# Second buffers for the first block's softmax, an early table load, and two new figures in a list scheduler

## The chip, the cores and the metric

The kernel runs on one core of one Trainium2 chip. A core has a matrix engine (PE, with its weight loads PEld), a vector engine (DVE), a scalar engine (ACT), a general engine (POOL) and a sync engine (SP) that here issues every transfer between device memory and the on-chip memory. Each engine executes its own instructions in the order in which they were written. The metric is the device time of one execution in microseconds (us); lower is better.

## What is computed

Three stages follow each other on 8 sequences of 576 tokens with 512 features, all in float32:

```python
# 1: attention inside chunks of 64 tokens, 8 heads of 64
scores = (q_c @ k_c.T) / 8;  attn = softmax(scores);  x = attn @ v_c
# 2: gated MLP with a convolution over the tokens
h = relu(x @ w_in)                      # 512 -> 1024
h = h * sigmoid(conv3(h, conv_w))
x = h @ w_out                           # 1024 -> 512
# 3: Fourier mixing, norm, MLP
u = x + real(fft over tokens and features of x)
out = u + relu(norm(u) @ w_ch1) @ w_ch2 # 512 -> 2048 -> 512
```

## The kernel before

**The stages.** The 4608 tokens are cut into ten blocks, of 256, eight times 512, and 256 tokens. For each block `attention(i, q, ...)` computes the heads in two halves, q = 0 and q = 1, and `values` multiplies by V; then come eight feature groups f, each with an `m_step` (times `w_in`, relu, convolution, gate) and an `x_step` (times `w_out`). Finished sequences are folded and transformed (`fold`, `d_step`, `s_step`, `u_step`). About 560 us into the execution the first two stages end, and two long stretches of matrix products for stage three follow (`group` with line L946, `second` with line L1010).

**The weights.** They arrive as 64-bit words in which two 32-bit words stand for one number, 512 KB for one group. `load_weight` loads the 16 groups of `w_in` and `w_out` in turn into five landing buffers (names `dd`, `fw`, `wide` in the trace), and `to_float32` turns each into float32 with one ACT multiplication (L293) and three DVE operations (L294, L295, L296). For the first block the float32 weights are used as they are (L460, L532); later blocks use a split into a high and a low part (L280 on ACT, L281 on DVE).

**The softmax of one half.** PE makes the scores (L393); DVE takes the maxima (L398) and scales them (L399) into `mx`; ACT computes the exponentials row by row into `es`, with sums into `sm` (L404); DVE adds a small number to the sums (L408), takes reciprocals (L409) and multiplies (L410); PE transposes `es` (L419), ACT copies the result to `at` (L422); PE multiplies by V (L436), ACT copies that out (L443). In the kernel before, `es`, `mx` and `sm` have one buffer each, so the second half's exponentials are written where the first half's were.

**The order of the work.** No order is written out. Every step is given to a `Plan` with an engine, an assumed cost, a priority number and the buffers that it reads and writes. `Plan.emit` is a list scheduler: it keeps an assumed clock for each engine, picks the next step by earliest start and then by priority, and emits the instructions of each engine in that order. The order is fixed before the kernel runs; at run time the engines wait for each other by semaphores alone. Two figures in it:

```python
o.end = t + o.cost * (2 if e == "PE" and t < self.COLD else 1)     # PE at double cost up to COLD ns
...
moved = max(o.end + 1500, moved) + o.nbytes / 280                  # all transfers in one row, 280 bytes per ns
o.lat = moved + 300 - o.end
```

`cv` is a pair of buffers of the convolution, 512 columns wide, used in turn by the `m_step`s.

Of the kernel before, what the change touches and what calls it, by code (L numbers as in the profile page):

```python
# [8 lines left out]
F32 = mybir.dt.float32  # L9
# [3 lines left out]
ACT = mybir.ActivationFunctionType  # L13
# [88 lines left out]
class Plan:  # L102


    CROSS = 200.0
    COLD = 30000.0
    SAME = {"DVE": 125.0, "ACT": 150.0}
    ANY_ORDER = ("o", "sum")

# [3 lines left out]
    def buf(self, pool, tag, bufs, shape, dtype=F32):  # L113
        return Buf(self, pool, tag, bufs, shape, dtype)
# [41 lines left out]
    def emit(self):  # L156
        clock, ready = {}, {}
        free = {tag: [0.0] * ring[0].bufs for (_, tag), ring in self.rings.items() if tag in self.ANY_ORDER}

        def push(o):  # L160
            ready.setdefault(o.eng, []).append(o)
            clock.setdefault(o.eng, 0.0)

        def start(o):
            t = max(o.ready, clock[o.eng])
            if o.slots:
                f = free[o.slots[0].tag]
                n = len(o.slots) + o.spare
                t = max(t, f[n - 1]) if len(f) >= n else float("inf")
            return t  # L170

        for o in self.ops:
            if not o.left:
                push(o)
        done, moved = 0, 0.0
        while True:
            best = None
            for e, ops in ready.items():
                if ops:
                    t = min(start(o) for o in ops)  # L180
                    if best is None or t < best[0]:
                        best = (t, e)
            if best is None:
                break
            t, e = best
            o = min((o for o in ready[e] if start(o) <= t), key=lambda o: (o.prio, o.seq))
            ready[e].remove(o)
            for b in o.slots:
                free[b.tag].pop(0)
            o.end = t + o.cost * (2 if e == "PE" and t < self.COLD else 1)  # L190
            clock[e] = o.end
            o.lat = 0.0
            if o.nbytes:
                moved = max(o.end + 1500, moved) + o.nbytes / 280
                o.lat = moved + 300 - o.end
            o.fn()
            done += 1
            for b in o.held:
                b.left -= 1
                if not b.left:  # L200
                    free[b.tag].append(o.end + o.lat + self.CROSS)
                    free[b.tag].sort()
            for u in o.users:
                if u.deps[o]:
                    u.ready = max(u.ready, o.end + o.lat + (self.CROSS if u.eng != e else self.SAME.get(e, 0.0)))
                else:
                    u.ready = max(u.ready, t)
                u.left -= 1
                if not u.left:
                    push(u)  # L210
        assert done == len(self.ops), (done, len(self.ops))
        return max(clock.values())
# [15 lines left out]
def kernel(  # L228
# [15 lines left out]
    pe, dve, act, pool, sp = nc.tensor, nc.vector, nc.scalar, nc.gpsimd, nc.sync  # L244
    plan = Plan()
    buf, op = plan.buf, plan.op
# [4 lines left out]
    const = ctx.enter_context(tc.tile_pool(name="const", bufs=1))  # L251
# [4 lines left out]
    pools["s"] = tc.alloc_tile_pool(name="seq", bufs=1, side="right")  # L256

    ident = const.tile([128, 128], F32, name="ident")

    def dram_buf(name, cols=512):  # L260
        b = buf("dram", name, 1, None)
        b.tile = dram.tile([128, cols], F32, name=name, tag=name)
        return b
# [6 lines left out]
    def load(dst, src, nbytes, prio, r=(), after=()):  # L270
        return op("SP", 450, lambda: sp.dma_start(out=dst(), in_=src()), prio, r=r, w=[dst], after=after, nbytes=nbytes)

    def vop(n, fn, prio, r, w, fast=False, scalars=0):
        return op("DVE", dve_cost(n, fast, scalars), fn, prio, r=r, w=w)

    def aop(n, fn, prio, r, w, psum=False, scalars=0, after=()):
        return op("ACT", act_cost(n, psum, scalars), fn, prio, r=r, w=w, after=after)
# [93 lines left out]
    def attention(i, q, prio, last):  # L371
        nw = SIZE[i] // 256
        n = 4 * nw
        blk = AT[i] // 256
        half = (slice(0, 64), slice(64, 128))
        qks, v = [], []
        for p in range(2):
            qks.append(buf(*(("s", "xlo", 2) if i + q == 1 and not i else ("a", "qk", 2)), [128, nw, 2, 256]))
            load(qks[p], lambda p=p: qk[blk:blk + nw, 2 * q + p].rearrange("w r a t -> r w a t"), 262144 * nw, prio - 12 + p)
        for p in range(2):  # L380
            v.append(buf("a", "v", 4, [128, nw, 256]))
            load(v[p], lambda p=p: v_in[blk:blk + nw, 2 * q + p].rearrange("w r t -> r w t"), 131072 * nw, prio - 10 + p)

        s = [buf("ps", "o" if i else "x", 4, [128, n, 64]) for _ in range(2)]

        def qk_unit():
            for w in range(nw):
                for j in range(2):
                    for p in range(2):
                        for u in range(2):  # L390
                            for h in range(2):
                                t, ks = qks[p](), slice(64 * (2 * j + u), 64 * (2 * j + u) + 64)
                                pe.matmul(s[h]()[half[u], 4 * w + 2 * p + j, :], t[half[h], w, 0, ks], t[half[h], w, 1, ks], start=True, stop=True)  # L393

        op("PE", 310 + 470 * nw, qk_unit, prio, r=qks, w=s)
        es, mx, sm = buf("a", "es", 1, [128, 2 * n, 64]), buf("a", "mx", 1, [128, 2, n]), buf("a", "sm", 1, [128, 2 * n, 1])
        for h in range(2):
            vop(64 * n, lambda h=h: dve.tensor_reduce(out=mx()[:, h, :], in_=s[h](), op=ALU.max, axis=AX.X), prio, [s[h]], [mx])  # L398
        vop(2 * n, lambda: dve.tensor_scalar(mx(), mx(), -0.125, None, op0=ALU.mult), prio, [mx], [mx])  # L399

        for h in range(2):
            def exp(ks, h=h):
                for k in ks:
                    act.activation(out=es()[:, n * h + k, :], in_=s[h]()[:, k, :], func=ACT.Exp, scale=0.125, bias=mx()[:, h, k:k + 1], accum_out=sm()[:, n * h + k, :])  # L404

            for ks in (range(k, k + 4) for k in range(0, n, 4)):
                op("ACT", 291 * 4, lambda exp=exp, ks=ks: exp(ks), prio, r=[s[h], mx], w=[es, sm])
        vop(2 * n, lambda: dve.tensor_scalar(sm(), sm(), 1e-9, None, op0=ALU.add), prio, [sm], [sm])  # L408
        vop(2 * n, lambda: dve.reciprocal(out=sm(), in_=sm()), prio, [sm], [sm])  # L409
        vop(128 * n, lambda: dve.tensor_tensor(es(), es(), sm().to_broadcast([128, 2 * n, 64]), op=ALU.mult), prio, [es, sm], [es])  # L410

        at = buf("a", "at", 2, [128, n, 128])
        for c in range(nw):
            tps = buf("ps", "o", 4, [128, 4, 128])

            def tr_unit(c=c, tps=tps):
                flat = es().rearrange("p a k -> p (a k)")
                for k in range(4):
                    pe.transpose(tps()[:, k, :], flat[:, 512 * c + 128 * k:512 * c + 128 * k + 128], ident)  # L419

            op("PE", 436, tr_unit, prio + 2, r=[es], w=[tps], spare=1)
            aop(512, lambda c=c, tps=tps: act.copy(out=at()[:, 4 * c:4 * c + 4, :], in_=tps()), prio + 2, [tps], [at], True)  # L422

        return lambda: values(i, q, nw, v, at, last)
# [616 lines left out]
    for q in range(2):  # L1041
        attention(0, q, -10 + q, -6 + q)()
# [8 lines left out]
    for i in range(NBLK):  # L1051
        t, u, step = place(i, 0), place(i + 1, 0) if i + 1 < NBLK else 0, SIZE[i] / 288
        if i + 1 < NBLK:
            rest = [attention(i + 1, q, *((t + (u - t) * (0.05 + 0.4 * q), u - 1.5 + 0.3 * q) if i else (t - 3.5 + 3 * q, t + 0.5 + 3 * q))) for q in range(2)]
            if not i:
                heads(1)
                for finish in rest:
                    finish()
# [54 lines left out]
    for c in range(NCH):  # L1113
        t = start + span * c
        begun = []
        for g in range(FG):
            begun.append(group(c, g, t + 7 * g))
            if (c, g) in LATE:
                n = LATE.index((c, g))
# [8 lines left out]
            second(c, j, t + 7 * (TILE0[c] // 2 + j), c + j == 0, c == NCH - 1 and j == HT[c] - 1)  # L1128

    with tc.manual_schedule():  # L1130
        make_identity(nc, ident)
        plan.emit()
        pools["e"].tile([128, 24], F32, tag="pad", name="pad", bufs=1)
        pools["e"].release()
        pools["b"].release()
# [109 lines left out]
```

## Time and profile before

| | |
|---|---|
| median of 3 runs | 1303.25 us (1302.99 to 1304.23) |
| time of the profiled execution | 1303.06 us |
| span of the profiled execution, first to last instruction | 1301.3 us |
| PE busy | 1274.9 us (98% of the span) |
| PEld busy | 1106.4 us (85%) |
| DVE busy | 1036.1 us (80%) |
| ACT busy | 761.4 us (59%) |
| granted PE clock, mean | 0.999 of full speed |
| moved by transfers | 206.16 MB |

Busy time is the time in which an instruction of that engine was executing; the rest of the span the engine waited or had nothing to do. An engine that is busy nearly all the span sets the time, and the places where it is not busy are where time could be saved.

### The profile page before, as it was taken

What the parts mean: (1) busy time and instruction counts of PE and PEld (TensorE: products, weight loads), DVE (VectorE), ACT (ScalarE), POOL (GpSimd) and SP (SyncE); (2) the same over time, 40 slices, a digit from 0 to 9 for tenths busy, and PEclk for the clock granted to TensorE, in tenths of its full rate; (3) what the DMA queues carried; (4) which work ended last, traced back from release to release, by engine and by line L of the source; (5) the groups of instructions that cost most, each with busy time, mean ns of one, the idle gap of its engine ahead of it and who ended that gap; (6) DMA issues with size and microseconds to landing.
All of it is one profiled execution on the core that took longest, in us unless ns stands there. A gap on an engine that the chain in (4) does not pass through costs nothing.

```text
span 1301.3 us, 24089 instructions
## 1 busy us (share of the span) xinstructions
PE 1274.9 (98%) x8880; PEld 1106.4 (85%) x8880; DVE 1036.1 (80%) x1909; ACT 761.4 (59%) x1902; POOL 112.3 (9%) x247
## 2 busy tenths in 40 slices
PE   5899999999999999999999999999999999999998
PEld 4788888888888888999999888888888888888887
DVE  5998878888786877887977757664599998998995
ACT  6887666768676665666756556566644334334331
POOL 0131212121030312210000000000000000000000
PEclk9999999999999999999999999999999999999999
DMA  9535242534413132258674866778655554554541
GB/s 339 178 108 175 78 129 90 187 100 158 135 57 103 34 98 62 63 172 267 203 238 144 255 182 204 214 238 273 200 159 165 176 168 146 173 171 141 174 140 41
DMA packets 155319, 206.16 MB, mean 158 GB/s; under 512 B 10304, under 2 KB 103104, under 8 KB 155200
## 3 DMA queue, kind: packets, MB, share of 16 engines
q1 hardware_dynamic: 155200, 204.61, 49.7%
q8 instruction: 70, 1.15, 0.4%
q14 instruction: 49, 0.40, 0.1%
HBM read 130.51 MB, written 74.06 MB: 157 GB/s over the span
## 4 chain that ended last, share of the span: by engine, by line
PE 93%; DVE 5%; ACT 1%; issue 1%; DMA 0%; SPq 0%; DVEq 0%; ACTq 0%
PE x L946 21%; PE x L1010 15%; PE x L538 15%; PE o L469 14%; PE o L1010 12%; PE o L946 4%; PE o L672 3%; PE o L705 2%; PE o L727 1%; PE o L436 1%; PE o L393 1%; PE o L844 1%; PE o L419 1%; ACT es L404 1%; DVE cv L489 0%
## 5 line engine op out<-in xcount | busy, mean ns | idle before, releaser
L946 PE MATMUL x<-sxh,t 128*128 128x512 f32 (+1 forms) x960 | 285.2, 369 | 1.1 <-ACT sum L929 0.6
L280 ACT CAST sxh<-raw 128x1024 fp32r<-128x1024 f32 (+1 forms) x143 | 144.9, 1029 | 201.7 <-DVE raw L856 84.3
L946 PEld LDWEIGHTS x<-sxh,t 128*128 128x128 f32 x960 | 177.9, 188 | 24.9 <-ACT sum L929 1.4
L946 PE MATMUL x<-sxl,t 128*128 128x512 f32 (+1 forms) x480 | 176.3, 367 | 0.0
L281 DVE TENSOR_TENSOR sxl<-raw,sxh 128x1024 fp32r<-128x1024 f32 (+1 forms) x143 | 168.7, 1192 | 9.5 <-ACT sxh L280 9.3
L469 PE MATMUL o<-x,wih 128*128 128x512 f32 (+1 forms) x576 | 172.2, 382 | 0.0
L489 DVE SCALAR_TENSOR_TENSOR cv<-h,cw,cv 128x512 f32<-128x512 f32 (+30 forms) x272 | 129.1, 495 | 31.9 <-ACT cv L499 31.6
L1010 PE MATMUL x<-t,sxh 128*128 128x512 f32 x576 | 144.4, 392 | 0.0
L469 PEld LDWEIGHTS o<-x,wih 128*128 128x128 f32 x576 | 104.6, 188 | 19.6
L1010 PEld LDWEIGHTS x<-t,sxh 128*128 128x128 f32 x576 | 103.7, 189 | 18.5
L538 PE MATMUL x<-gh,woh 128*128 128x512 f32 (+1 forms) x288 | 112.4, 390 | 0.0
L538 PE MATMUL x<-gh,wol 128*128 128x512 f32 (+1 forms) x288 | 109.3, 379 | 0.0
L538 PE MATMUL x<-gl,woh 128*128 128x512 f32 (+1 forms) x288 | 109.2, 379 | 0.0
L469 PE MATMUL o<-x,wil 128*128 128x512 f32 (+1 forms) x288 | 108.9, 378 | 0.0
L1010 PE MATMUL o<-t,sxh 128*128 128x512 f32 x432 | 108.3, 392 | 0.0
L946 PEld LDWEIGHTS x<-sxl,t 128*128 128x128 f32 x480 | 90.2, 188 | 11.2
L1010 PEld LDWEIGHTS o<-t,sxh 128*128 128x128 f32 x432 | 77.8, 189 | 13.9
L404 ACT ACTIVATE es<-o,mx 128x64 f32<-128x64 f32 x272 | 84.0, 358 | 8.9 <-DVE mx L399 8.9
L1030 DVE TENSOR_TENSOR u<-x,u 128x256 f32<-128x256 f32 x144 | 60.4, 422 | 29.9 <-PE x L1010 28.2
L856 DVE TENSOR_TENSOR raw<-raw 128x1024 f32<-128x1024 f32 (+1 forms) x70 | 84.0, 1202 | 0.1
L1010 PEld LDWEIGHTS x<-t,sxl 128*128 128x128 f32 x576 | 78.6, 190 | 5.6
L1010 PE MATMUL x<-t,sxl 128*128 128x256 f32 x576 | 80.5, 282 | 0.0
(263 smaller groups left out, 2394.1 us busy)
## 6 DMA issues: line engine op xcount, KB each, us to landing
raw<-h_scr SPq DMA_DIRECT2D x72, 512.0 KB, 4.6
h_scr<-sum SPq DMA_DIRECT2D x72, 256.0 KB, 3.3
u<-u_scr SPq DMA_DIRECT2D x66, 256.0 KB, 3.8
qk<-in_qk SPq DMA_DIRECT2D x32, 512.0 KB, 4.9
h_scr<-sum SPq DMA_DIRECT2D x48, 192.0 KB, 2.7
out_y<-u SPq DMA_DIRECT2D x35, 256.0 KB, 2.3
v<-in_v_in SPq DMA_DIRECT2D x32, 256.0 KB, 4.4
wide<-in_w_ch SPq DMA_DIRECT2D x16, 512.0 KB, 5.1
```

Source lines behind the costliest of these rows:

```text
L280: aop(n, lambda: act.copy(out=cut(h()), in_=cut(src())), prio, [src], [h], psum, after=after)
L281: vop(n, lambda: dve.tensor_tensor(cut(l()), cut(src()), cut(h()).bitcast(F32), op=ALU.subtract), prio, [src, h], [l])
L404: act.activation(out=es()[:, n * h + k, :], in_=s[h]()[:, k, :], func=ACT.Exp, scale=0.125, bias=mx()[:, h, k:k + 1], accum_out=sm()[:, n ...
L469: pe.matmul(acc(), w[:, ws], x, start=k == 0, stop=k == 11)
L489: vop(hi - lo, lambda: dve.scalar_tensor_tensor(cv()[:, lo:hi], in0=h()[:, off + k - 1 + lo:off + k - 1 + hi], scalar=tap(k), in1=cv()[:, ...
L538: pe.matmul(accs[d](), w[:, dsl], x, start=f == 0 and k == 0, stop=f == FT - 1 and k == 2)
L672: pe.matmul(acc()[:rows, :], x, w, start=k == 0 and n == 0, stop=k == 1 and n == 2)
L705: pe.matmul(accs[sine]()[:rows, :], w, x, start=n == 0, stop=n == len(todo) - 1)
L856: vop(n, lambda: dve.tensor_tensor(out(), x(), y(), op=alu), prio, r, w)
L946: pe.matmul(acc(), a, b, start=first and m == 0, stop=m == 5, skip_group_check=not first)
L1010: pe.matmul(acc()[:, :n], left[:, js], w()[:, cs], start=first and g == 0 and n == 512, stop=g == FG - 1 and n == 256, skip_group_check=True)
L1030: vop(256, lambda a=a, acc=accs[i], part=part, half=half: dve.tensor_tensor(part(us[a]()), acc()[:, half], part(us[a]()), op=ALU.add), t + ...
```

## The change

Four edits. The second half of the first block takes its `es` from the pair `cv` instead of the one buffer `es`; `mx` and `sm` get two buffers each, for all blocks. Ahead of everything else DVE writes zeros into a new column `unit` and ACT takes the exponential of it, so that ACT's function table is loaded there. In the scheduler, PE's steps count double up to 21000 ns of the plan instead of 30000, and transfers count at 330 bytes per ns instead of 280. The last two change no instruction, but the order in which all of them are emitted.

```diff
-    COLD = 30000.0
+    COLD = 21000.0
...
-                moved = max(o.end + 1500, moved) + o.nbytes / 280
+                moved = max(o.end + 1500, moved) + o.nbytes / 330
...
+    unit = const.tile([128, 1], F32, name="unit")
...
-        es, mx, sm = buf("a", "es", 1, [128, 2 * n, 64]), buf("a", "mx", 1, [128, 2, n]), buf("a", "sm", 1, [128, 2 * n, 1])
+        es, mx, sm = buf("a", *(("cv", 2) if i == 0 and q else ("es", 1)), [128, 2 * n, 64]), buf("a", "mx", 2, [128, 2, n]), buf("a", "sm", 2, [128, 2 * n, 1])
...
     with tc.manual_schedule():
+        dve.memset(unit, 0.0)
+        act.activation(out=unit, in_=unit, func=ACT.Exp)
         make_identity(nc, ident)
         plan.emit()
```

## Rows read from the trace of the kernel before

**Rows 1.** Windows: stretch, length, busy us (instructions) by engine, PE clock, DMA share, GB/s.
```profile
0.00:10.00 10.00, 2.82 (x64) 2.07 (x64) 0.99 (x4) 3.85 (x18) 0.70 (x6) 1.00 0.81 255
10.00:20.00 10.00, 5.18 (x70) 3.61 (x74) 7.39 (x21) 6.68 (x26) 0.00 (x0) 1.00 1.04 385
20.00:30.00 10.00, 7.23 (x103) 5.56 (x95) 9.50 (x20) 6.74 (x30) 0.57 (x1) 1.00 0.99 370
30.00:40.00 10.00, 8.43 (x157) 6.71 (x158) 8.06 (x19) 10.00 (x32) 0.88 (x3) 1.00 0.47 161
40.00:50.00 10.00, 8.36 (x37) 6.79 (x38) 10.00 (x23) 8.55 (x42) 0.65 (x1) 1.00 0.69 254
50.00:60.00 10.00, 9.24 (x163) 7.60 (x163) 10.00 (x20) 9.28 (x20) 3.28 (x3) 1.00 0.34 98
60.00:80.00 20.00, 19.99 (x94) 16.59 (x93) 20.00 (x42) 16.92 (x61) 7.71 (x9) 1.00 0.41 137
...
500.00:700.00 200.00, 196.80 (x1304) 190.11 (x1304) 154.16 (x339) 123.62 (x301) 14.74 (x44) 0.99 0.58 177
...
sum 1301.30, PE 1274.92 PEld 1106.44 DVE 1036.11 ACT 761.38 POOL 112.28; mean PE 70.83 PEld 61.47 DVE 57.56 ACT 42.30 POOL 6.24
```

**Rows 2.** Timeline, first 30 us: start, duration, engine, line, [idle before <- releaser].
```profile
5.09 0.76 DVE L398 TENSOR_REDUCE mx<-x 128x4 f32<-128x256 f32 x2 [5.09 <-PE x L393]
...
5.88 0.17 DVE L399 TENSOR_SCALAR mx<-mx 128x8 f32<-128x8 f32 x1
...
6.14 1.28 ACT L404 ACT_TABLE_LOAD   x1 [6.14 <-DVE mx L399]
...
6.78 0.92 PE L393 MATMUL x<-xlo 64*64 64x64 f32 x24 [0.57 <-DMA xlo<-in_qk]
...
9.94 0.17 DVE L408 TENSOR_SCALAR sm<-sm 128x8 f32<-128x8 f32 x1 [3.88 <-ACT es L404]
...
10.49 0.43 DVE L294 TENSOR_SCALAR t<-wx 128x512 uint32<-128x512 uint32 x1
...
11.77 0.68 DVE L295 SCALAR_TENSOR_TENSOR t<-dd,t 128x512 uint32<-128x512 uint32 x1
...
12.48 0.69 DVE L296 SCALAR_TENSOR_TENSOR t<-wx,t 128x512 uint32<-128x512 uint32 x1
...
12.79 0.31 ACT L404 ACTIVATE es<-x,mx 128x64 f32<-128x64 f32 x1 [2.33 <-PE o L419]
...
15.78 0.17 DVE L408 TENSOR_SCALAR sm<-sm 128x8 f32<-128x8 f32 x1 [2.60 <-ACT es L404]
...
16.29 0.69 DVE L410 TENSOR_TENSOR es<-es,sm 128x512 f32<-128x512 f32 x1
...
20.98 0.68 ACT L293 ACTIVATE wf<-dd 128x512 f32<-128x512 f32 x1
```

**Rows 3.** Timeline of DVE, 27 to 33 us: its two stalls there.
```profile
27.96 0.43 DVE L294 TENSOR_SCALAR f<-wx 128x512 uint32<-128x512 uint32 x1 [0.40 <-ACT wx L293]
...
32.08 0.17 DVE L408 TENSOR_SCALAR sm<-sm 128x16 f32<-128x16 f32 x1 [1.91 <-ACT es L404]
```

**Rows 4.** Timeline of the SP queue: the sixth weight's load issues (start, duration).
```profile
12.51 0.34 SPq L271 DMA_DIRECT2D dd<-in_w_out  x1
```

**Rows 5.** DMA issues, 12.5 to 12.8 us: count, size, us to landing.
```profile
dd<-in_w_out SPq DMA_DIRECT2D x1, 512.0 KB, 6.8
```

**Rows 6.** PE by line and form, up to 21 us and from 21 us: busy, mean ns.
```profile
L460 PE MATMUL o<-gl,t 128*128 128x256 f32 x4 | 2.4, 714 | 0.0
...
L460 PE MATMUL o<-gl,u 128*128 128x256 f32 x8 | 1.9, 379 | 0.0
```

**Rows 7.** Windows of 10 us around the change of stages, columns as in rows 1.
```profile
560.00:570.00 10.00, 8.34 (x60) 7.91 (x59) 8.07 (x20) 3.84 (x16) 1.64 (x1) 0.89 0.14 52
570.00:580.00 10.00, 9.46 (x69) 9.11 (x68) 9.50 (x20) 9.21 (x20) 3.15 (x16) 0.94 0.40 120
...
590.00:600.00 10.00, 10.00 (x65) 9.89 (x64) 7.48 (x13) 4.91 (x12) 0.00 (x0) 1.00 0.94 306
```

## The prediction

> **What bounds the kernel now.** I read the windows first. PE is busy 1274.92 of 1301.30 us, so all its idle time is 26.4 us, and nothing in the change takes a matrix product away: the change can only move those 26.4 us. The windows say where they lie [rows 1]: PE is busy 2.82, 5.18, 7.23, 8.43, 8.36 and 9.24 of the first six stretches of 10 us, which is 18.7 us of idle time before 60 us; from 60 to 80 us it is busy 19.99 of 20; from 500 to 700 us it lacks 3.2 us. So 18.7 of 26.4 us are lost while the kernel starts up, and the reader should ask who holds PE up there.
>
> The same rows answer it. From 20 us on DVE is busy 9.50, 8.06, 10.00, 10.00 and then 20.00 of 20: it is full of weight conversions and splits, and PE starves behind it until about 60 us. DVE's own idle time before that is what counts: a microsecond of it saved brings everything behind it, and so PE's full load, forward by a microsecond. The timeline shows its stalls [rows 2]: 5.09 us until the first scores (needed: nothing has landed), 3.88 us until the exponentials of the first half are done, 2.60 us until those of the second half are done, and later 0.40 and 1.91 us [rows 3].
>
> **The table load.** Before, ACT loads its table at 6.14, after the maxima are there, for 1.28 us, and the exponentials run to DVE's row at 9.94, that is 2.5 us from the load's end at 7.42 [rows 2]. With the load ahead, in the first 5 us where ACT has nothing, they run from 6.14 to 8.64. The added zeros and the one exponential are hidden in the same empty 5 us; without that cover they would cost a small DVE row (0.17) and one ACT row (0.31) [rows 2].
> The row shows no more than 1.28 us, with the first exponential right behind it (6.14 + 1.28 + 2.5 = 9.92). The Trainium skill, "ScalarE: Activation LUTs", section "What ACT_TABLE_LOAD costs", gives the same load 1283 ns but adds a drain of about 1380 ns for a switch. By that page 1.38 us more would be saved and the sum below would be 1298.8 instead of 1300.2; the trace of this kernel has no idle stretch where that drain would be.
>
> **The own buffers.** Before, the second half's exponentials start at 12.79, released by PE's transposes of the first half (2.33 us of ACT idle), because both halves share `es`; DVE then waits for them until 15.78 [rows 2]. With own `es`, `mx` and `sm` they depend on their scores alone: PE ends these at 6.78 + 0.92 = 7.70; two reductions take 0.76, to 8.46; scaling takes 0.17 and a hand-over of 0.09 (5.88 + 0.17 to 6.14) follows: 8.72 [rows 2]. That is just after the first half's 8.64. They end 2.5 us later, and DVE starts on the sums at about 11.25. From the sums to the end of the multiplication it took 16.29 + 0.69 - 15.78 = 1.20 us: 12.45 instead of 16.98.
>
> One thing goes the other way. Before, ACT used its wait for the first weight's multiplication, and DVE converted that weight in its own gap, with 0.43 + 0.68 + 0.69 = 1.80 us of rows from 10.49 on [rows 2]. Now ACT is taken by exponentials of better priority until 11.2, and the 1.80 us come behind 12.45: 14.25. Small rows for the convolution's weights, which before hid inside the 15.78 to 16.29 stretch, are between 0 and that 0.51 us; I take 0.2, as they are of the size of the 0.17 rows and partly overlap. So the state that DVE had reached at 16.98 it reaches at 14.45: **2.5 us sooner**.
>
> Does the data let it? The queue of transfers is full from 10 to 30 us (DMA share 1.04 and 0.99 [rows 1]), so loads cannot come much earlier. The tightest is the sixth weight: issued at 12.51 when its landing buffer came free, landed 6.8 later at 19.3 [rows 4, 5], multiplied at 20.98 [rows 2]. Moved forward by 2.5 it is wanted at 18.5, 0.8 too early. That 0.8 is the most that it can take from the gain if DVE has nothing else then; I count 0, as its weight belongs to a later product. Behind SP's wait for that buffer stand the loads of the next block's V and of further weights; the buffer is now freed by a conversion that comes up to 1.4 us later (12.45 + 0.43 + 0.68 against 11.77 + 0.68), but a load that takes 6.8 us to land at a share of 1.04 lies behind others that were issued before it [rows 1, 5], so the queue does not run dry in 1.4 us.
>
> The `cv` slot that `es` borrows is wanted again by the second feature group's convolution, whose product needs weights converted after the first one's 14.25; its readers, the transposes, come right behind 12.45; its cost is 0. The second `mx` and `sm` of later blocks free DVE and ACT from waits while PE is full anyway (19.99 of 20 [rows 1]): 0.
>
> **The two figures.** They only reorder. PE's rows for one form take 714 ns up to 21 us and 379 ns after [rows 6], so a double cost up to 21 us of the plan fits these rows better than up to 30; the granted clock in those windows is shown as 1.00, the 2.4 GHz level, all the time [rows 1], so it is the durations that I go by. Transfers moved 385 and 370 GB/s in the start [rows 1], so 330 fits better there than 280, and 306 GB/s at share 0.94 in a later full stretch [rows 7], where 330 is too much. What a better order gives lies between 0 and DVE's remaining stalls of 0.40 + 1.91 = 2.31 us [rows 3]. The 1.91 is DVE waiting for the next block's exponentials, and no edit shortens those; the 0.40 is a weight multiplication that stood behind exponentials on ACT, which is now 2.5 us ahead. I take 0.4.
>
> **The sum.** 2.5 + 0.4 = 2.9 us off the profiled execution's own 1303.06 us (1.76 us of it lie outside the span): **1300.2 us**. The median of the runs, 1303.25, is 0.2 above that execution, so this is 0.23% below it. Differences under 0.2% (2.6 us) can hardly be told from none for this kernel. Its own bounds: 2.5 - 0.8 gives 1301.4, and 2.5 + 2.31 gives 1298.3.
>
> **Rivals.**
> *More is won.* The new order also removes PE waits between 30 and 60 us, which lack 1.57 + 1.64 + 0.76 = 3.97 us [rows 1]. All of DVE's 2.31 gives 1298.3, half of the 3.97 on top 1296.3. For it: these waits come from an order made with figures that do not fit the start. Against it: DVE is already full from 40 us.
> *Hidden by the transfers.* If the full queue, and not DVE, paces the weights, only the start of the first softmax moves, and at most the 1.28 of the table is left: 1301.8 to 1303.1. For it: shares of 1.04 and 0.99 [rows 1]. Against it: the sixth weight lay 1.7 us before it was used, and DVE's stalls name ACT, not a transfer [rows 2, 3].
> *Slower: loads planned too early.* From 500 to 700 us 177 GB/s for 200 us are 35.4 MB. Planned at 330 they take 107.3 us, at the 306 of the full stretch 115.7: 8.4 us late if all came in one go, 4.9 at the measured share of 0.58 [rows 1, 7]. Instructions in order behind a late load stop PE. Around 560 us the rows show what such a stop brings: 1.66 + 0.54 us idle, and a clock of 0.89 and 0.94 of the 2.4 GHz level after it, another 1.1 + 0.6 us [rows 7]. So 4.9 + 1.7 - 2.9 = 3.7 us more than before: 1306.8. It turns the sign from 2.9 us on. Against it: DVE and ACT lack work there (154 and 124 of 200 us), so there is slack [rows 1].
> The Trainium skill, "DMA: Bandwidth & Descriptors", section "Specifications", puts the memory limit of a core at about 358 GB/s; by it 330 would be no overestimate and this rival would fall away, while the 306 of the row speaks for it, and the 385 of the start is above the page's limit.
> *The longer table load.* Were 1.38 us more hidden in the stretch before the first exponential than its load row shows, the time would be 1298.8. The row at 9.94 leaves no room for it. This is the page's drain above.
>
> **Chances.** The forecast 0.44, more won 0.18, hidden 0.24, slower by late loads 0.12, longer load 0.02. About three quarters of the forecast's own range lies below 1300.65 (0.2% under the median): 0.33 + 0.18 + 0.02 = 0.53 faster; 0.11 + 0.24 and 0.02 of the late loads = 0.37 the same; 0.10 slower. The range leaves out the lower half of "more won" and the late loads: 1297.0 to 1303.6.
>
> **What would show it.** Right: the table load below 3 us, the second half's exponentials directly behind the first's and ending near 11.2, the multiplication into `es` of the second half ending near 12.5, the first weight's conversion after it, and 2.9 us less PE idle time before 60 us (15.8 instead of 18.7), with the rest shifted as a whole. Wrong: a stall of DVE or ACT on a weight's transfer between 15 and 30 us, the 1.91 us stall grown by as much as was won, PE idle between 60 and 500 us, or more idle time and a lower clock between 560 and 640 us.

## The result, and the profile after

The kernel after takes **1317.06 us** (median of 5 runs, 1315.37 to 1320.51) against 1303.25 (1302.99 to 1304.23) before: the ratio is **1.0107, 95% interval 1.0091 to 1.0123**. It is slower by 1.1%, where 1300.2 had been forecast, a small gain. The profiled execution is the longest of the five, 1320.51 us with a span of 1318.7.

First the same windows of the kernel after that [rows 1] show of before (stretch, length, busy us and instructions by engine, PE clock, DMA share, GB/s):

```profile
0.00:10.00 10.00, 2.82 (x64) 2.07 (x64) 2.72 (x10) 4.75 (x23) 0.70 (x6) 1.00 0.78 243
10.00:20.00 10.00, 7.36 (x108) 4.99 (x111) 8.38 (x21) 7.01 (x24) 0.00 (x0) 1.00 1.04 394
20.00:30.00 10.00, 7.78 (x80) 6.59 (x73) 8.47 (x17) 7.97 (x38) 0.56 (x3) 1.00 1.05 392
30.00:40.00 10.00, 9.59 (x164) 7.63 (x163) 9.25 (x21) 10.00 (x33) 0.20 (x1) 1.00 0.65 220
40.00:50.00 10.00, 7.30 (x94) 5.72 (x94) 9.92 (x21) 10.00 (x39) 0.67 (x2) 1.00 0.80 281
50.00:60.00 10.00, 8.94 (x100) 7.00 (x99) 10.00 (x22) 8.30 (x27) 1.78 (x2) 1.00 0.50 158
500.00:700.00 200.00, 193.82 (x1262) 184.09 (x1261) 151.65 (x339) 122.71 (x308) 14.64 (x45) 0.98 0.55 170
```

PE is busy 43.79 us before 60 us, against 41.26 before [rows 1]: 2.5 us of waiting are gone, close to the forecast's 2.9. In size, the start brought nearly what was expected of it. The loss must lie behind 60 us, and it is about 20 us in this execution.

The next question is whether it is waiting or work. The first line of the page (busy time, share of the span, instructions) of the kernel after:

```profile
PE 1291.4 (98%) x8880; PEld 1108.6 (84%) x8880; DVE 1037.6 (79%) x1910; ACT 762.6 (58%) x1903; POOL 112.1 (9%) x247
```

PE was busy 1274.92 before [rows 1] and is busy 1291.4 now, 16.5 us more, in a span that is 17.4 us longer; its idle time is 27.3 us against 26.4. No product was added. So nearly all of the loss is time in which PE is busy: the same products take longer. Which ones? The groups of PE by line (line, operation, operands, shape, count, then busy us, mean ns of one, and idle us just ahead of them), of the kernel before, chosen rows:

```profile
L946 PE MATMUL x<-sxh,t 128*128 128x512 f32 (+1 forms) x960 | 285.2, 369 | 1.1 <-ACT sum L929 0.6 <-DVE u L921 0.4
L946 PE MATMUL x<-sxl,t 128*128 128x512 f32 (+1 forms) x480 | 176.3, 367 | 0.0
L469 PE MATMUL o<-x,wih 128*128 128x512 f32 (+1 forms) x576 | 172.2, 382 | 0.0
L1010 PE MATMUL x<-t,sxh 128*128 128x512 f32 x576 | 144.4, 392 | 0.0
L538 PE MATMUL x<-gl,woh 128*128 128x512 f32 (+1 forms) x288 | 109.2, 379 | 0.0
```

and of the kernel after (its lines from 259 on stand one number higher):

```profile
L947 PE MATMUL x<-sxh,t 128*128 128x512 f32 (+1 forms) x960 | 289.5, 373 | 2.8 <-ACT sum L930 2.1 <-ACT u L930 0.6
L947 PE MATMUL x<-sxl,t 128*128 128x512 f32 (+1 forms) x480 | 178.5, 372 | 0.0
L470 PE MATMUL o<-x,wih 128*128 128x512 f32 (+1 forms) x576 | 174.5, 386 | 0.1
L1011 PE MATMUL x<-t,sxh 128*128 128x512 f32 x576 | 145.8, 395 | 0.0
L539 PE MATMUL x<-gl,woh 128*128 128x512 f32 (+1 forms) x288 | 110.2, 383 | 0.2 <-DVE gl L282 0.2
```

In every large group a product takes 3 to 5 ns longer, in all stages. The reader is to see that this is spread evenly: a wait would sit in one place. The chain of waits says the same in runs of equal products (start, us, count). Before:

```profile
241.83 8.16 PE o L469 x36
...
780.11 8.16 PE x L946 x36
...
973.50 2.79 PE o L1010 x16
```

and after:

```profile
241.43 8.36 PE o L470 x36
...
762.43 8.40 PE x L947 x36
...
812.04 8.16 PE x L947 x36
...
975.21 2.81 PE o L1011 x16
```

36 products one behind the other took 8.16 us, 226.7 ns each; now they take 8.36 and 8.40 us, 232 and 233 ns each. But one run of L947 still takes 8.16: the slow pace belongs to some operands of a line, not to the line or to a stretch of time.

The starts of single products, read from the traces (us; the differences are taken before rounding), say where in the execution the time is lost (one kernel of the experiments below stands beside them):

```
                                     before    after    difference   e4_after_placed
first product at L469 (after: L470)    61.0     58.9      -2.1         58.5
last product at L538 (L539)           562.3    567.4      +5.1        560.7
first product at L946 (L947)          577.1    582.2      +5.1        575.5
241st product at L946                 629.2    640.7     +11.4        631.1
last product at L946                  950.8    966.4     +15.6        953.1
last product at L1010 (L1011)        1297.2   1314.7     +17.4       1299.5
```

From 61 to 562 us the kernel after loses 7.2 us, in one stretch of 52 us alone 6.3, and then 6.0 to the end. The stretch of 6.3 holds something else too, a stretch at a lower clock. Two windows of the kernel after (columns as above), in which the mean clock stands at 0.83 of its 2.4 GHz level; the second lies in the stretch of 6.3:

```profile
570.00:580.00 10.00, 8.34 (x55) 8.00 (x54) 9.50 (x25) 5.90 (x17) 4.81 (x16) 0.83 0.14 53
...
630.00:640.00 10.00, 8.42 (x39) 7.73 (x38) 7.31 (x19) 5.52 (x11) 0.00 (x0) 0.83 0.71 234
```

A mean of 0.83 over 10 us is 3.4 us at the 1.2 GHz level, at most 1.7 us of lost work. Before, there was one such stretch, shared by two windows at 0.89 and 0.94 [rows 7]; after, there are two. The one between the last product at L538 and the first at L946 costs nothing: these two are 14.8 us apart before and after, and as far apart in run 4 below, which has no such stretch. So only the second, at 634.2 us, adds to the loss.

### The profile page after: what moved, and what is told of

Its sections match the earlier page's. It is cut to its first block, busy times and chain, and to the rows that moved or that the text cites. A ratio compares the mean times of both kernels' runs of the same rounds, so it can differ in the third digit from the quotient of the medians.

```text
span 1318.7 us, 24082 instructions
## 1 busy us (share of the span) xinstructions
PE 1291.4 (98%) x8880; PEld 1108.6 (84%) x8880; DVE 1037.6 (79%) x1910; ACT 762.6 (58%) x1903; POOL 112.1 (9%) x247
## 4 chain that ended last, share of the span: by engine, by line
PE 83%; DVE 7%; ACT 4%; DMA 4%; issue 1%; POOL 0%; SPq 0%; ACTq 0%; DVEq 0%; POOLq 0%
PE x L947 20%; PE x L1011 15%; PE x L539 12%; PE o L1011 12%; PE o L470 11%; PE o L947 3%; PE o L673 3%; PE o L706 2%; DVE cv L490 2%; ACT es L405 1%; PE o L728 1%; PE o L845 1%; PE o L437 1%; PE o L394 1%; PE o L420 1%
## 5 line engine op out<-in xcount | busy, mean ns | idle before, releaser
L947 PE MATMUL x<-sxh,t 128*128 128x512 f32 (+1 forms) x960 | 289.5, 373 | 2.8 <-ACT sum L930 2.1
L947 PEld LDWEIGHTS x<-sxh,t 128*128 128x128 f32 x960 | 179.1, 189 | 29.8 <-ACT sum L930 2.8
L947 PE MATMUL x<-sxl,t 128*128 128x512 f32 (+1 forms) x480 | 178.5, 372 | 0.0
L470 PE MATMUL o<-x,wih 128*128 128x512 f32 (+1 forms) x576 | 174.5, 386 | 0.1
L490 DVE SCALAR_TENSOR_TENSOR cv<-h,cw,cv 128x512 f32<-128x512 f32 (+31 forms) x272 | 128.7, 494 | 41.1 <-ACT cv L500 40.8
L1011 PE MATMUL x<-t,sxh 128*128 128x512 f32 x576 | 145.8, 395 | 0.0
L470 PEld LDWEIGHTS o<-x,wih 128*128 128x128 f32 x576 | 104.6, 189 | 21.7 <-DVE x L446 0.4
L1011 PEld LDWEIGHTS x<-t,sxh 128*128 128x128 f32 x576 | 103.2, 188 | 19.2
L539 PE MATMUL x<-gh,woh 128*128 128x512 f32 (+1 forms) x288 | 113.2, 393 | 0.0
L539 PE MATMUL x<-gl,woh 128*128 128x512 f32 (+1 forms) x288 | 110.2, 383 | 0.2 <-DVE gl L282 0.2
L539 PE MATMUL x<-gh,wol 128*128 128x512 f32 (+1 forms) x288 | 110.2, 382 | 0.0
L470 PE MATMUL o<-x,wil 128*128 128x512 f32 (+1 forms) x288 | 110.0, 382 | 0.0
L1011 PE MATMUL o<-t,sxh 128*128 128x512 f32 x432 | 109.5, 395 | 0.0
L947 PEld LDWEIGHTS x<-sxl,t 128*128 128x128 f32 x480 | 90.6, 189 | 12.5
L1011 PEld LDWEIGHTS o<-t,sxh 128*128 128x128 f32 x432 | 77.4, 188 | 14.6
L1011 PEld LDWEIGHTS x<-t,sxl 128*128 128x128 f32 x576 | 78.3, 188 | 6.5
L1011 PE MATMUL x<-t,sxl 128*128 128x256 f32 x576 | 79.9, 280 | 0.0
```

Source lines behind the costliest of these rows:

```text
L470: pe.matmul(acc(), w[:, ws], x, start=k == 0, stop=k == 11)
L490: vop(hi - lo, lambda: dve.scalar_tensor_tensor(cv()[:, lo:hi], in0=h()[:, off + k - 1 + lo:off + k - 1 + hi], scalar=tap(k), in1=cv()[:, ...
L539: pe.matmul(accs[d](), w[:, dsl], x, start=f == 0 and k == 0, stop=f == FT - 1 and k == 2)
L947: pe.matmul(acc(), a, b, start=first and m == 0, stop=m == 5, skip_group_check=not first)
L1011: pe.matmul(acc()[:, :n], left[:, js], w()[:, cs], start=first and g == 0 and n == 512, stop=g == FG - 1 and n == 256, skip_group_check=True)
```

## The theory, and what the edits do to the memory

The one edit that touches what these products read is the allocation of buffers. Every tile gets its place in the on-chip memory from the allocations ahead of it. In the built programs `unit` takes 32 bytes of each partition and shifts all tiles allocated from its side: `wih` from 9856 to 9888, `sxh` from 26240 to 26272. Stage three has sixteen `t` tiles in eight groups of two: those of three groups move by 32 as well, while those of the other five, allocated from the far side, stay, or move by a multiple of 256. The second `mx` and `sm` add 128 bytes more ahead of `x`, `gh` and `gl`: `x` goes from 125568 to 125728. So the distance changes between the tile that a product streams (`x`, `gh`, `gl`, `sxh`, `t`: the first operand in the rows) and the weights loaded for the next product. Before, this distance was a multiple of 256 bytes for all products of 512 columns at these four lines that are followed by one of the same line. The starts of the trace's products, sorted by the distance (address of the streamed operand less that of the next weights, modulo 256), give the mean step from one product to the next of its line; steps of 260 ns and more, which hold a wait or the lower clock, are left out:

```
line, 512 columns        before: distance: ns (products)    after: distance: ns (products)
L469 (L470) o<-x,wih     0: 227.6 (695)                     128: 232.3 (696)
L538 (L539) x<-gh,woh    0: 228.7 (646)                     128: 232.6 (654)
L946 (L947) x<-sxh,t     0: 227.1 (986)                     0: 227.5 (371)   32: 233.3 (619)
L1010 (L1011) x<-t,sxh   0: 230.1 (1008)                    0: 231.3 (377)  224: 233.1 (630)
```

For 21 products at L947 their own weights and the next ones lie differently: 12 with 0 to their own and 32 to the next step by 235.0 ns, 9 with 32 and 0 by 229.6; in run 2 below it is 234.5 and 230.4. Few as they are, they point to the next weights.

**The theory, placement:** the tiles' new places make the products slower, by this distance. **A first rival, loads:** the figure of 330 lets loads of stage three be planned too early, as in the prediction's slower rival. **A second, the clock:** the longer steps are a lower clock that the record does not show, brought by new gaps. Kernels that move tiles and change nothing else tell placement from both.

## The experiments

Each ratio is to the kernel before on the same chip, with a 95% interval. There are ten kernels.

**Run 1: 128 bytes ahead of the first block's tiles, nothing else** (`e1_pad128`).

```diff
         make_identity(nc, ident)
+        pools["a"].tile([128, 32], F32, tag="pad", name="pad", bufs=1)
         plan.emit()
```

> The kernel before, with one unused column of 128 bytes per partition at the start of the pool heads; no instruction and no order changes, but every tile of that pool (x0, gh, gl and others) lies 128 bytes higher against the weights wih, wil, woh, wol. Theory placement: a float32r product of 512 columns takes longer when the distance between its moving operand and the next product's weights is not a multiple of 256 bytes; in the changed kernel the two lines concerned stepped at 232 instead of 227 ns at a distance of 128. So 1536 products by 5 ns: 7.7 us more, about 1310.9 us, with steps of 232 ns in the first two stages and 227 ns in the first half of stage three. Rival order: the slowdown of the changed kernel comes from the order that the scheduler's new figures make; then this is 1303.3 us.

Measured: 1308.44 us (1308.31 to 1310.12) against 1302.77, ratio 1.0043 (1.0030 to 1.0055). The step is 232 ns at L469 and L538 and 227 at L946, as placement says; the time is 5.7 us longer instead of the 7.7 that 1536 products at 5 ns would make. In the profiled execution, the longest of the five, it is 5.0 us from the first product at L469 to the last at L538 (506.3 against 501.3), as not every step is longer by 5 ns, and another 1.2 from the first to the 241st at L946 (53.3 against 52.2), where the pace is the old one and ACT waits longer for transfers. The chain of waits of this kernel has the same slow piece as the kernel after:

```profile
243.87 8.37 PE o L469 x36
```

An unused tile of 128 bytes makes the kernel 0.4% slower. Neither rival can have made the steps longer here: no load and no order has changed, and the mean granted clock of this execution is 1.000.

**Run 2: the column `unit` alone** (`e2_unit32`).

```diff
+    unit = const.tile([128, 1], F32, name="unit")
...
+        dve.memset(unit, 0.0)
```

> The kernel before, with the new column unit allocated and zeroed, and nothing else; it takes 32 bytes, by which all tiles on the left side of the memory move, those on the right side stay. Theory placement: the first two stages keep 227 ns, as operands and weights move together; in group, five of eight groups have weights on the right and operands on the left, 630 products by 6.5 ns and 420 shorter ones by 1.7 ns, 4.8 us, and in second about 2.2 us (126 halves at 2.81 instead of 2.79 us): 1310 us. Rival order: 1303.3 us.

Measured: 1309.58 us (1309.09 to 1310.68), ratio 1.0049 (1.0036 to 1.0062). Its chain shows the old pace where both operands moved together, and the new one at L947:

```profile
241.73 8.16 PE o L470 x36
...
760.98 8.39 PE x L947 x36
```

The steps are 227 ns at L470 and L539, 227 and 234 at L947 for the distances 0 and 32, and 233 at L1011 for 224. The two parts add up: 0.43% and 0.49% here, and 0.91% by which the kernel after exceeds run 4 (1317.06 over 1305.2), which has the change without them.

**Run 3: 256 bytes instead of 128** (`e3_pad256`).

```diff
+        pools["a"].tile([128, 64], F32, tag="pad", name="pad", bufs=1)
```

> As the run with 128 bytes, but 256 bytes. Theory placement, with 256 bytes as the period: steps of 227 ns in all stages up to group, 1303.3 us. Rival: any move of these tiles costs (or a longer period, or a place where the memory's ports are shared), then as with 128 bytes, about 1311 us. Rival order: 1303.3 us.

Measured: 1303.16 us (1302.63 to 1303.89), ratio 0.9999 (0.9991 to 1.0008). Twice the padding costs nothing:

```profile
241.69 8.16 PE o L469 x36
```

So it does not matter that a tile moves, but by how much, and the amount of memory taken is no reason either.

**Run 4: the whole change, its tiles put back** (`e4_after_placed`). The zeros and the exponential use the first column of `ident`, which is written right behind them, and 128 unused bytes fill up the heads' 128 to 256.

```diff
-    unit = const.tile([128, 1], F32, name="unit")
+    unit = ident[:, :1]
...
+        pools["a"].tile([128, 32], F32, tag="pad", name="pad", bufs=1)
         plan.emit()
```

> The changed kernel with all its edits, but placed as before: the early exponential works on the first column of ident, so that no new column moves anything, and 128 unused bytes at the start of heads make the distance that the second mx and sm add up to 256. Theory placement: the 14.7 us of longer steps go; what stays is 0.9 us more idle time of PE and 3.4 us more at the half clock (1.7 us): 1305.7 us, or as low as 1300.2 us if those came from the longer steps too. Rival order: still about 1317 us.

Measured: 1305.2 us (1304.09 to 1306.66) against 1302.77, ratio 1.0016 (1.0007 to 1.0025). All steps are back at 227 to 230 ns, and 11.9 us of the 13.8 lost have returned: placement is the greater part. The order of the products is that of the kernel after, so the steps of the two traces can be compared one by one: from 61 us on, the products of 512 columns at a changed distance are shorter by 3.4 us in total at L470, 2.9 at L539, 3.9 at L947 and 2.8 at L1011 (steps under 300 ns), 13.0 of the 15.1 us between the two executions. But the start's gain does not show: the time is 2.4 us above before, not 2.9 below. This kernel's column in the table of starts says where the gain goes. At 61 us it is 2.5 us ahead, at 562 us still 1.6; from the first to the 241st product at L946 it needs 55.6 us where before needed 52.2, for the same 310 products, and there the lead turns into a lag of 1.8. The waits of ACT from 560 to 660 us (line, waited for: us in total, times, longest) show the first rival in that place:

```profile
ACT t L281 <- DMA ts<-t_scr: 3.1, 2, 2.2
...
ACT sxh L281 <- DMA raw<-first_scr: 2.0, 1, 2.0
```

Before, the same view has no wait for `t_scr`, and 0.3 us for `first_scr`. PE waits for ACT in turn. Its waits from 575 to 660 us (same columns), in the kernel before and in run 4:

```profile
PE x L946 <- ACT sum L929: 0.6, 1, 0.6
...
PE x L947 <- ACT sum L930: 1.8, 2, 1.2
```

Two windows of PE alone (busy us, products, PE clock, DMA share, GB/s), of the kernel before:

```profile
580.00:590.00 10.00, 10.00 (x69) 1.00 0.89 287
...
620.00:630.00 10.00, 9.57 (x60) 1.00 1.03 310
```

and the same of run 4, with all engines:

```profile
580.00:590.00 10.00, 9.35 (x58) 8.65 (x57) 8.52 (x15) 6.15 (x12) 0.00 (x0) 1.00 0.71 254
...
620.00:630.00 10.00, 8.79 (x50) 8.15 (x49) 7.97 (x19) 6.37 (x14) 0.00 (x0) 1.00 0.91 302
```

**Run 5: the same with the old figures** (`e5_edits_old_figures`), so buffers and table load alone, placed.

```diff
-    COLD = 21000.0
+    COLD = 30000.0
...
-                moved = max(o.end + 1500, moved) + o.nbytes / 330
+                moved = max(o.end + 1500, moved) + o.nbytes / 280
```

> The changed kernel placed as before (as in the run after_placed), with the old figures 280 and 30000 in the scheduler: own buffers and early table load alone. Theory: what is left of the slowdown, once the placement is mended, is stage three waiting for transfers that the scheduler believes to move at 330; with 280 those waits go and the start's gain of 2.5 to 2.9 us remains: about 1300.2 us, with products in group beginning about 2.5 us sooner than before and no ACT wait for a transfer between 575 and 610 us. Rival: the own buffers' order itself loses the later time; then 1303 to 1305 us.

Measured: 1302.81 us (1300.78 to 1304.44) against 1303.32, ratio 0.9995 (0.9986 to 1.0003). ACT has no wait for `t_scr` here. The last product at L539 starts at 561.3, 1.0 us ahead of before. The time says that less is gained than the 2.5 us forecast for the buffers: the interval allows 1.8 at most. It does not say that the buffers bring less by themselves, for the profile has 3.4 us at 1.2 GHz at 32.3 us, in the start, which can hide up to 1.7 us of a gain; the mean clock of its eleven executions is 0.9973, where that of the executions of before beside them is 0.9987.

**Run 6: 330 at the start, 280 from 500 us of the plan on** (`e6_rate_by_stage`), all else as in run 4.

```diff
-                moved = max(o.end + 1500, moved) + o.nbytes / 330
+                moved = max(o.end + 1500, moved) + o.nbytes / (330 if t < 500000.0 else 280)
```

> The changed kernel placed as before, with 330 bytes per ns up to 500 us of the plan and 280 after. Theory late loads in stage three: the start's gain of 2.5 us stays and the loss between 575 and 640 us goes: 1300.3 us or less. Rival: the loss comes from how the start's order shifts everything, whatever the rate is later; then 1305 us as in after_placed.

Measured: 1301.82 us (1301.36 to 1303.21) against 1303.32, ratio **0.9986 (0.9977 to 0.9996)**. This is the one version whose interval lies below before, by 0.14%. Its profile is of its longest execution and doesn't show the gain: the last product starts at 1297.4, 0.1 later than before. Of ACT's two waits the one for `t_scr` is gone but for a remainder, and the one for `first_scr` has stayed, which marks the first as the cost of the later figure:

```profile
ACT sxh L281 <- DMA raw<-first_scr: 2.1, 1, 2.1
...
ACT t L281 <- DMA ts<-t_scr: 0.2, 1, 0.2
```

From the first to the 241st product at L947 this kernel needs 53.2 us instead of 55.6. The 1.0 us that is left over before goes with the wait for `first_scr`, which the figure doesn't make: runs 1 and 10, with the order of before, have 2.3 and 1.8 us of it and need 53.3 and 52.9 us there, runs 2, 3 and 7 have at most 0.9 and need 52.1 to 52.2. The ratio is 0.30% below that of run 4, 3.9 us, which is more than these 2.4; where the rest comes from is not shown.

**Run 7: the table load alone** (`e7_table_only`).

```diff
+        dve.memset(ident[:, :1], 0.0)
+        act.activation(out=ident[:, :1], in_=ident[:, :1], func=ACT.Exp)
         make_identity(nc, ident)
```

> The kernel before with the early table load alone, on the first column of ident; the order of all else is that of before. Theory: the first exponentials start 1.28 us sooner and everything behind them follows: 1301.5 us. Rival, the drain that the Trainium skill's page on ScalarE states beside the load: 2.66 us, 1300.1 us. Rival, hidden: the transfers pace the start, 1302.8 us.

Measured: 1303.22 us (1301.88 to 1305.59), ratio 0.9999 (0.9991 to 1.0008). Nothing is gained. The timelines of ACT and of DVE (start, us, what; in brackets the idle time before it and what ended it) say why:

```profile
10.21 0.66 ACT L293 ACTIVATE wx<-dd 128x512 f32<-128x512 f32 x1 [1.56 <-DMA dd<-in_w_in]
```

```profile
10.90 0.43 DVE L294 TENSOR_SCALAR t<-wx 128x512 uint32<-128x512 uint32 x1 [1.60 <-ACT wx L293]
11.24 0.68 DVE L410 TENSOR_TENSOR es<-es,sm 128x512 f32<-128x512 f32 x1
```

DVE has the first half's sums at 8.69 instead of 9.94 [rows 2], 1.25 us sooner, but in its fixed order the first weight's conversion stands ahead of the multiplication into `es`, and that weight lands at 10.2. The gain runs into a transfer and is lost in this order.

**Run 8: the two figures alone** (`e8_figures_only`).

```diff
-    COLD = 30000.0
+    COLD = 21000.0
...
-                moved = max(o.end + 1500, moved) + o.nbytes / 280
+                moved = max(o.end + 1500, moved) + o.nbytes / 330
```

> The kernel before with the figures 330 and 21000 alone; the placement is unchanged. Theory late loads: the start may gain up to 1 us, and stage three loses about 3.5 us to waits for transfers between 575 and 640 us: about 1305.5 us. Rival: the figures fit better and gain by themselves, 1300 to 1302 us.

Measured: 1305.12 us (1303.28 to 1306.66), ratio 1.0011 (1.0002 to 1.0020). In the profile, which is of its fastest execution, the first product at L469 starts at 58.2 us, 2.8 sooner than before and sooner than in any other run. ACT then waits 2.8 us for `t_scr`, and the last product starts at 1297.5, 0.2 later than before. So the figures, costed at 0.4 us, bring about as much at the start as all edits together, and lose it in stage three.

**Run 9: the figure for a cold PE alone** (`e9_cold_only`).

```diff
-    COLD = 30000.0
+    COLD = 21000.0
```

> The kernel before with 21000 in place of 30000 and nothing else. Theory (the bandwidth figure brings the loads of stage three too early, the figure for a cold TensorE only orders the first 30 us): no wait of ACT for t or ts on a transfer between 560 and 660 us beyond the 2 us on raw that the kernel before has there; from the first product of stage three to its 240th as in before, 52.1 us; time 1301.5 to 1303.5. If the early loads come from the cold figure instead, ACT waits for t by 2 to 3 us as in the run with both figures and the time is 1304 to 1306.

Measured: 1305.65 us (1304.69 to 1307.35) against 1303.30, ratio 1.0017 (1.0008 to 1.0026). Half of the expectation held: ACT does not wait for `t_scr`, so waits as long as those of runs 4 and 8 belong to 330. But the time is 2.3 us longer instead of the same. PE's idle time before 60 us is 18.8 us, nothing won, and the first product at L469 starts 1.5 us later than before, with 3.4 us at 1.2 GHz ahead of it (window of PE):

```profile
50.00:60.00 10.00, 7.76 (x150) 0.83 0.09 18
```

Another 0.8 us comes between the first and the 241st product at L946 (53.0 instead of 52.2 us), with 1.9 us of ACT waiting for `first_scr`, as in run 6. That 21000 fits the durations of [rows 6] better does not make the order that comes of it better.

**Run 10: 64 bytes** (`e10_pad64`).

```diff
+        pools["a"].tile([128, 16], F32, tag="pad", name="pad", bufs=1)
```

> The kernel before with 64 bytes of padding ahead of the first block's tiles, so that the left operands of the products at L469 and L538 lie 64 bytes, modulo 256, from their weights. Theory (the step between two products depends on that distance and is 227 ns at 0 only): a step of 232 to 234 ns at L469 and L538 and 1308 to 1311 us. If only distances that are no multiple of 64 cost anything beside 128, the step stays at 227 ns and the time at 1303.

Measured: 1304.95 us (1304.26 to 1305.99) against 1303.30, ratio 1.0010 (1.0001 to 1.0019). Both expectations missed: the step is 229 to 230 ns at L469 and L538, between the two.

```profile
241.99 8.24 PE o L469 x36
```

## Why the prediction was wrong

**The step that failed** is in the own buffers: the second `mx` and `sm` of later blocks were costed at 0, with PE "full anyway", and of `unit` only the zeros and the exponential were costed. Where the new tiles lie, and what they move, was not costed at all. That term decides. Run 4 differs from after by placement alone and takes 11.9 us less; between their two profiled executions it is 15.1 us at the last product. The table of starts divides these: from the first product at L470 to the last at L539 after takes 508.5 us and run 4 502.2, so 6.3; from the 241st product at L947 to the last 325.7 and 322.0, so 3.7; from there to the last at L1011 348.3 and 346.5, so 1.8; from the first to the 241st at L947 58.4 and 55.6, so 2.9, of which up to 1.7 is the stretch at 1.2 GHz around 636 us; and 0.4 at the start. The forecast treated PE's 1274.92 us of busy time as fixed, since "nothing in the change takes a matrix product away". None was added either, and still it grew by 16.5 us.

**The start came out near its size, by another order.** Timeline rows of after, of ACT:

```profile
0.73 1.28 ACT L1133 ACT_TABLE_LOAD   x1 [0.73 <-PEq L1235]
2.03 0.20 ACT L1133 ACTIVATE unit<-unit 128x1 f32<-128x1 f32 x1
...
10.39 0.68 ACT L294 ACTIVATE wx<-dd 128x512 f32<-128x512 f32 x1
```

and of DVE:

```profile
12.36 0.68 DVE L297 SCALAR_TENSOR_TENSOR t<-wx,t 128x512 uint32<-128x512 uint32 x1
...
13.76 0.69 DVE L411 TENSOR_TENSOR cv<-cv,sm 128x512 f32<-128x512 f32 x1
```

ACT multiplied the first weight between exponentials of the second half, not behind them, so the weight's conversion was done at 13.04, before the multiplication into `cv`, which ends at 13.76 + 0.69 = 14.45. That is the very time forecast for the state that DVE had reached at 16.98; but the multiplication was to end near 12.5 and the conversion to come behind it, so the agreement to the hundredth is luck. The stall of 1.91 us [rows 3] stayed, at 1.64. PE's idle time before 60 us fell by 2.5 us, and by 2.8 in run 4, where 2.9 were forecast.

The clock of 1.00 that the prediction read for the first windows is no reading: the trace's record of the granted clock begins only at 21.7 us before, and a window without a record shows 1.00. In run 5 the products of 256 columns at L461 step by 427 ns ahead of its first record, at 18.7 us, and by 216 from 21 us on, so the pace was half at first. It was right to go by the durations; that a double cost up to 21 us then makes a better order was not (run 9).

**Who brings it was wrong.** The buffers were given 2.5 us and the figures 0.4. Run 8 gives the figures alone 2.8 at 61 us and 1.4 at 562; all together (run 4) reach 2.5 and 1.6. Run 5 gives buffers and table load 1.0 us by 562 us, with up to 1.7 hidden by the lower clock. So the gains overlap, and part of a lead at 61 us is gone at 562; the buffers' own share stays open.

**"With the rest shifted as a whole" failed.** The rival of loads planned too early, given 0.12, is what became of the start's gain: ACT waits for `t_scr` for 4.7 us in the kernel after, 3.1 in run 4 and 2.8 in run 8, with 330, and for 0 to 0.9 us in all others, with 280 in that stage. The price was put at 4.9 + 1.7 us; in run 4 it is 3.4 (55.6 against 52.2), with no stretch at 1.2 GHz in that place, and run 6 takes 2.4 of it back. The 306 GB/s of [rows 7] pointed the right way. By the limit of about 358 GB/s in the Trainium skill, "DMA: Bandwidth & Descriptors", section "Specifications", 330 would have been no overestimate, and the rival void.

**The longer table load is void as well.** In the rows above, the first exponential starts at 2.03, where the load of 1.28 us ends, and in run 7, with the load out of the way, the first half's sums come 1.25 us sooner, the length of the load and no more. The drain of about 1380 ns that the Trainium skill, "ScalarE: Activation LUTs", section "What ACT_TABLE_LOAD costs", adds to a switch does not show in this trace.

**What stays open:** why the step depends on the distance (0, 32, 64, 128 and 224 bytes modulo 256 were met, each with a few pairs of tiles); what makes the wait for `first_scr` in stage three longer or shorter; what the buffers bring by themselves; and which waits bring the stretches at 1.2 GHz.

## What to carry to other kernels

When PE is busy for 98% of the span, compare the mean duration of its largest groups before and after, and not the waits alone: a change that adds any tile, even one column, can move all tiles behind it, and 2% on each product is more than a start can win. Cost a new allocation by what it moves, keep the distances that gave the best pace (here multiples of 256 bytes, for products of 512 columns), and test for it with a kernel that allocates and does nothing else. A planner's bandwidth is a figure for a stretch: read it from the fullest windows of each, since one that fits the start can cost later what it won.

## What the runs showed of the hardware

**The pace of a matrix product depends on where its operands lie.** The median step between two products of 512 columns, by the distance of the streamed operand from the next product's weights modulo 256: 227 ns at 0 (229 to 230 at L1010), 229 to 230 at 64 (run 10), 232 at 128 (after and run 1), 233 at 224 and 234 at 32 (after and run 2), all at the 2.4 GHz level. Shorter products differ: between the kernel after and run 4, those of 384 columns at L947 are 1.4 ns longer at 32, and those of 256 columns at L1011 1.6 ns shorter at 224, where products with an unchanged distance differ by about 1 ns as well. The Trainium skill, "TensorE: Matmul & The Clock Gate", section "Wait — 56ns, not 53.3ns?", gives 215.7 ns from start to start for 512 columns, with no condition on addresses. The smallest median here is 227 (the shortest single steps are 224), and addresses alone move it by 3%.

**The stretch at 1.2 GHz wanders, and its price depends on the place.** 3.4 us at the lower level stand at 567.8 us before and in run 3, at 567.4 in run 6, at 572.8 and 634.2 after, at 30.7 in run 2, 32.3 in run 5, 52.7 in run 9, and nowhere ahead of the end in runs 1, 4, 7, 8 and 10. Around 570 us, where PE waits, it costs next to nothing (14.8 to 14.9 us from the last product at L538 to the first at L946 with it, 14.8 without it); where PE is full it is up to 1.7 us, more than the 1.5 us that the best version wins, so a gain of this size needs the median of many executions. It is not chance alone: the mean clock over eleven executions is 0.9973 in run 5 and 0.9997 in run 8.
